# The first chunk's w_down product as seven products for eight, its sums on VectorE between the gate steps

## The chip, the cores and the metric

One NeuronCore of a Trainium2 chip runs the whole kernel. The metric is the time of one execution on the device in microseconds. Engines in the profile: PE is the tensor engine (PEld its weight loads), DVE is VectorE, ACT is ScalarE, POOL is GpSimd, SP the queue that issues most transfers. PE writes its results into banks of PSUM, from which the other engines take them.

## The reference, cut to what matters

```
xn = layernorm(x)                          # x: 2048 x 448
q  = xn @ wq                               # 16 heads of 256
s  = softmax(q k^T / 16) v  @ wo           # 512 keys, 8 kv heads
g  = silu((gelu(xn @ w_gate) * (xn @ w_up)) @ w_down)     # 1792 features
return x + s * g                           # bf16
```

The change touches only `(gelu(..) * (..)) @ w_down`: 2048 x 1792 by 1792 x 448, done in four chunks of 512 rows.

## The kernel before

The gate part is a loop of steps; a step makes two blocks of 128 features for 512 rows on PE (28 matmuls), then ScalarE takes the gelu and VectorE the multiply out of PSUM. Chunk 0 has steps 0 to 12, chunk 1 steps 14 to 26, and so on. Between steps stands a chunk's product with w_down. Three of the four chunks do it already as a 2 x 2 block product with seven block products for eight (Winograd's form): some block sums first, seven products, then combinations.

```python
def down(c, pairs):                      # chunk 0: the plain product, bf16
    for t4 in range(4):
        ...
        mms([(bank[b][:, 0:D], actT[:, c % 2, f, t4 * P:(t4 + 1) * P], wd[:, f, :], f == 0, f == NF - 1)
             for f in range(NF)], [b_wd] + b_actT[c % 2], (b_ps[b],))
        act(tmp[:, s, 0:D], bank[b][:, 0:D], ACT.Tanh, ..., scale=0.5)
        ...                              # gate on VectorE, store

def sum_wd(o, x, y):                     # one of four weight sums, 128 x 1568, fp16
    add("dve", wdt[o][0], wdt[x][0], wdt[y][0], ..., ALU.subtract)

def sum_act(c, k, i=None):               # one of four activation sums, in two halves i of feature blocks
    ...                                  # k = 0 is in place: right half of the rows becomes left - right

def down7(c, banks, g, b_g, order=(3, 6, 5, 4, 2, 1), then=None):
    ...
    A = lambda e, r: (lambda i: actTh[:, c % 2, e * NH + i, r * HC:(r + 1) * HC], b_actT[c % 2][e * NH:(e + 1) * NH])
    ...
    product(0, B1, A(0, 0))              # 14 matmuls of 128 x 224 each
    act(U2, bank[B1][:, 0:D], ACT.Copy, (b_ps[B1],), bU2, scale=F)
    for j in order:
        product(j, *what[j], j != 1)
    if then:
        then()
    plus(U2, bU2, B6, U2, bU2)           # six combinations on VectorE, then tanh and gate
    ...
```

Note the second element of `A(0, 0)`: the buffers that the first product is said to read are those of whole feature blocks, while it reads the left half of their rows.

The softmax here doesn't subtract the row's maximum and nothing guards it: scores larger than these inputs give would overflow.

## Time and profile before

| | us |
|---|---|
| median of 3 runs (lowest to highest) | 541.97 (541.92 to 542.07) |
| PE busy | 533.5 of a span of 540.6 |
| chunk 0: plain product, first matmul to next step | 10.70 |
| chunk 1: seven products, first matmul to next step | 9.49 |

PE is the bound from end to end; the prediction shows the lines. For stages I use three landmarks on PE: the first whole gate step (its first matmul on w_gate's last rows), the first attention product, and the last run of matmuls with w_o. Before, these stand at 12.02, 119.03 and 531.19 us. The profile's view of busy time in the two stretches between them (length; busy us and instructions of PE, PEld, DVE, ACT, POOL; clock; DMA share; GB/s):

```profile
12.02:119.03 107.01, 106.83 (x962) 55.79 (x960) 78.21 (x146) 60.66 (x95) 14.35 (x27) 1.00 0.61 137
119.03:531.19 412.16, 410.00 (x2883) 237.69 (x2907) 284.20 (x632) 246.01 (x672) 23.61 (x44) 1.00 0.50 104
```

I call them **head** (107.01 us) and **attention part** (412.16 us); the change edits only the head.

### The profile page before, as it was taken

The page shows a single profiled execution, that of the slowest core. Times are in us where ns is not written, and L with a number is a line of the kernel's source. Part 1 is how long each engine was busy: PE and PEld are TensorE (multiplying, and loading weights), DVE is VectorE, ACT ScalarE, POOL GpSimd, SP SyncE. Part 2 cuts the span into 40 slices and gives each one's busy share as a digit, 9 for nine tenths or more (in the row PEclk, how much of TensorE's full clock was granted, in tenths as well). Part 3 has the DMA queues.
Part 4 walks back from the last instruction along what each step waited for, and adds up shares of the span by engine and source line. Part 5 has one row for each costly group of instructions (what it writes and reads, how often), then busy time and mean ns, then how long its engine had stood idle before and what let it go on. Part 6 is the DMA issues. An engine that isn't in the chain of part 4 may idle for free.

```text
span 540.6 us, 10823 instructions
## 1 busy us (share of the span) xinstructions
PE 533.5 (99%) x4113; PEld 306.1 (57%) x4138; DVE 376.2 (70%) x825; ACT 313.3 (58%) x780; POOL 39.4 (7%) x78
## 2 busy tenths in 40 slices
PE   8999999999999999999999999999999999999997
PEld 5554457449644444984444469544444984444587
DVE  6673895799767757934875786367567934776775
ACT  5433854873658858116875860488488116876820
POOL 1130400000000010003001000120100003001010
PEclk9999999999999999999999999999999999999999
DMA  9569271921496788302781670076457402873731
GB/s 291 128 186 130 45 142 41 299 66 41 113 191 133 147 192 156 60 1 78 166 145 47 156 137 1 18 148 149 94 106 153 64 1 72 162 156 83 134 72 35
DMA packets 171604, 61.38 MB, mean 114 GB/s; under 512 B 155104, under 2 KB 168416, under 8 KB 171552
## 3 DMA queue, kind: packets, MB, share of 16 engines
q1 hardware_dynamic: 167488, 51.30, 44.5%
q0 software_dynamic: 3008, 8.72, 7.1%
q8 instruction: 33, 0.54, 0.4%
q10 hardware_dynamic: 1056, 0.66, 0.4%
q14 instruction: 19, 0.16, 0.1%
HBM read 19.76 MB, written 3.67 MB: 43 GB/s over the span
## 4 chain that ended last, share of the span: by engine, by line
PE 98%; issue 0%; DMA 0%; DVE 0%
PE bank L392 98%; DMA x<-in_A_x_dram 0%; DVE stats L439 0%; PE bank L490 0%; DVE xn L465 0%; DVE mv L442 0%; PE bank L509 0%; DVE xnT L898 0%; DVE xnT L386 0%; DVE rstd L459 0%
## 5 line engine op out<-in xcount | busy, mean ns | idle before, releaser
L844 ACT ACTIVATE p<-bank 128x512 f32<-128x512 f32 x256 | 150.6, 596 | 27.8 <-DVE pn L851 25.4
L392 PE MATMUL bank<-pT,va 128*128 128x512 bf16 x512 | 120.9, 379 | 0.0
L392 PE MATMUL bank<-kT,qT 128*128 128x512 bf16 x487 | 117.8, 379 | 2.3 <-ACT qT L383 1.0
L851 DVE TENSOR_SCALAR pn<-p,rden 128x512 bf16<-128x512 f32 x256 | 113.0, 483 | 8.2 <-DMA pT<-pn 3.9
L392 PE MATMUL bank<-xnT,wq 64*128 64x512 bf16 x768 | 94.9, 376 | 0.0
L392 PEld LDWEIGHTS bank<-kT,qT 128*128 128x128 bf16 x512 | 49.3, 98 | 61.7 <-issue 3.4
L392 PEld LDWEIGHTS bank<-pT,va 128*128 128x128 bf16 x512 | 49.6, 98 | 61.0 <-DMA pT<-pn 2.3
L392 PE MATMUL bank<-xnT,wgu 64*128 64x512 bf16 (+2 forms) x768 | 83.9, 350 | 0.1
L383 ACT ACTIVATE qT<-bank 128x512 bf16<-128x512 f32 x76 | 44.1, 596 | 51.8 <-PE bank L392 50.2
L829 DVE CAST qT<-bank 128x512 bf16<-128x512 f32 x52 | 34.8, 690 | 49.5 <-PE bank L392 49.5
L392 PEld LDWEIGHTS bank<-xnT,wq 64*128 64x128 bf16 x768 | 36.7, 94 | 46.3 <-ACT p L844 2.1
L392 PEld LDWEIGHTS bank<-xnT,wgu 64*128 64x128 bf16 x768 | 37.0, 94 | 36.8 <-issue 0.6
L848 DVE RECIPROCAL rden<-rsum 128x2 f32<-128x2 f32 x128 | 21.1, 165 | 47.0 <-ACT p L844 47.0
L844 ACT ACTIVATION_READ_ACCUMULATOR p<-bank 128x1 f32 x256 | 51.7, 202 | 0.0
L392 PE MATMUL bank<-wt,sr 128*128 128x224 f16 x512 | 50.0, 259 | 0.0
L383 ACT ACTIVATE gl<-bank 128x512 bf16<-128x512 f32 x56 | 33.1, 596 | 28.5 <-PE bank L392 26.1
L392 PEld LDWEIGHTS bank<-wt,sr 128*128 128x128 f16 x512 | 49.0, 98 | 0.4 <-ACT oTh L383 0.2
L869 DVE TENSOR_SCALAR oTh<-bank 128x512 f16<-128x512 f32 x62 | 42.3, 683 | 0.0
L383 ACT ACTIVATE oTh<-bank 128x512 f16<-128x512 f32 x66 | 38.9, 590 | 4.2 <-PE bank L392 4.2
L392 PE MATMUL bank<-wt,oTh 128*128 128x224 f16 (+1 forms) x416 | 38.4, 252 | 0.0
L392 PEld LDWEIGHTS bank<-wt,oTh 128*128 128x128 f16 x416 | 37.2, 98 | 0.9
L377 POOL DMA_DIRECT2D g<-g_all x14 | 7.6, 540 | 379.2 <-DVE xnT L386 255.3
(82 smaller groups left out, 403.6 us busy)
## 6 DMA issues: line engine op xcount, KB each, us to landing
wtb<-in_A_wo_dram POOLq DMA_DIRECT2D x4, 896.0 KB, 11.1
wq<-in_A_wq_dram SPq DMA_DIRECT2D x2, 1536.0 KB, 7.1
va<-in_A_v_cache_dram SPq DMA_DIRECT2D x8, 256.0 KB, 5.7
pT<-pn SPq DMA_TRANSPOSE x128, 2.8
xr<-in_A_x_dram POOLq DMA_DIRECT2D x15, 112.0 KB, 2.3
wd<-in_B_w_down_dram SPq DMA_DIRECT2D x1, 1568.0 KB, 7.4
g<-g_all POOLq DMA_DIRECT2D x14, 112.0 KB, 2.3
out_dram<-xr POOLq DMA_DIRECT2D x12, 112.0 KB, 2.1
```

Of the source, the lines that this page charges most:

```text
L377: K.op(q, lambda e, o=o, i=i: e.dma_start(o, i), reads, writes, dma=True, after=after)
L383: K.op("act", lambda e, o=o, i=i: e.activation(o, i, func, scale=scale), reads, writes)
L392: ins = e.matmul(o, lhsT=l, rhs=r, start=st, stop=sp, skip_group_check=True)
L829: K.op("dve", lambda v, s=s, b=b: v.tensor_copy(qT[:, s, 1, :], bank[b + 1]), (b_ps[b + 1],), (b_qT[s][1],))
L844: K.op("act", lambda e, b=b, r=r, z=z: e.activation(p32[:, z, :], bank[b], ACT.Exp, scale=att_scale, accum_out=rsum[:, r:r + 1]), (b_ps[b] ...
L848: K.op("dve", lambda e, r=r: e.reciprocal(rden[:, r - 1:r + 1], rsum[:, r - 1:r + 1]), b_rsum[r - 1:r + 1], b_rden[r - 1:r + 1])
L851: K.op("dve", lambda e, r=r - 1 + t, z=(n - 1 + t) % NP32, y=y, t=t: e.tensor_scalar(pn[:, y, t, :], p32[:, z, :], rden[:, r:r + 1], None, ...
L869: K.op("dve", lambda v, i=i, b=b: v.tensor_scalar(oTh[:, i, :], bank[b], WS, None, op0=ALU.mult), (b_ps[b],), (b_oT[i],))
```

## The change

Its intent: an eighth of the PE work of the last plain product goes, with the sums that this needs fitted into VectorE's free time between gate steps. The product moves from after step 18 to after step 26, so that the sums have time. The core of the diff:

```diff
-            o = actTh if c else actT
-            K.op("dve", lambda e: e.tensor_tensor(o[:, c % 2, f, :], bank[b + 1], gl[:, s, :], ALU.mult),
+            K.op("dve", lambda e: e.tensor_tensor(actTh[:, c % 2, f, :], bank[b + 1], gl[:, s, :], ALU.mult),
...
-        WD_CASTS = [(20, (j, e, n, i)) for ...]
-        DN_SUMS = [(24, sum_act, (1, k, 0)) for k in range(4)] + [
-            (30, sum_wd, x) for x in ((4, 4, 0), (5, 2, 4), (6, 5, 0), (3, 1, 5))] + [(34, sum_act, (1, k, 1)) for k in range(4)]
-        DOWN_AT = {NF + 5: 0, 39: 1}
+        WD_CASTS = [(16, (j, e, n, i)) for ...]
+        WD_SUMS = [(18, (4, 4, 0)), (20, (5, 2, 4)), (22, (6, 5, 0)), (24, (3, 1, 5))]
+        ACT_SUMS = [(n, (c, k, i)) for c, i, ns in ((0, 0, (10, 11, 19, 21)), (0, 1, (23, 23, 25, 25)),
+                                                    (1, 0, (30, 32, 34, 34)), (1, 1, (36, 36, 38, 38)))
+                    for k, n in enumerate(ns)]
+        DOWN_AT = {27: 0, 39: 1}
...
-            if ln_t[0] < 8 or n >= 12:
+            if ln_t[0] < 8 or 12 <= n and ln_t[0] < 12 or n >= 28:
                 ln_a()
...
-                    down(DOWN_AT[n + 1], cur)
+                def norms():
+                    for f in (ln_a, ln_a, ln_b, ln_b):
+                        f()
+                end = down7(DOWN_AT[n + 1], (...), (...), b_g2x, then=norms if n < 28 else None)
```

In a step the loop emits the weight sums of that step first and its activation sums after them.

## The prediction

> **What bounds the kernel now.** I read first the busy times and the chain that ended last, then the tensor engine's timeline around the product that is changed, then the vector engine's, because that is where the new work goes.
>
> The page of the kernel before (busy us, share of the span, instructions; then the chain by engine):
>
> ```profile
> PE 533.5 (99%) x4113; PEld 306.1 (57%) x4138; DVE 376.2 (70%) x825; ACT 313.3 (58%) x780; POOL 39.4 (7%) x78
> ...
> PE 98%; issue 0%; DMA 0%; DVE 0%
> ```
>
> The kernel is tensor-engine bound nearly from end to end. So a microsecond taken from PE's queue is a microsecond of time, unless PE then has to wait for somebody, and what another engine does costs nothing until PE waits for it. The tensor engine's timeline around the first chunk's w_down product (start, length, what), and around the second chunk's, which is already done as seven products:
>
> ```profile
> 36.53 1.48 PE L392 MATMUL bank<-xnT,wgu 64*128 64x512 bf16 x12
> 37.93 10.77 PE L392 MATMUL bank<-wd,actT 128*128 128x448 bf16 x56
> 48.63 0.82 PE L392 MATMUL bank<-xnT,wgu 64*128 64x512 bf16 x6
> ...
> 77.56 1.46 PE L392 MATMUL bank<-xnT,wgu 64*128 64x512 bf16 x12
> 78.96 1.52 PE L392 MATMUL bank<-wdh,actTh 128*128 128x224 f16 x14
> ...
> 88.45 0.82 PE L392 MATMUL bank<-xnT,wgu 64*128 64x512 bf16 x6
> ```
>
> From its first matmul to the first of the next gate step, the plain form takes 48.63 - 37.93 = 10.70 us and the seven-product form 88.45 - 78.96 = 9.49 us, neither with a wait in or ahead of it. Gate steps follow each other every 3.02 us (two feature blocks a step; step 18 ends at 37.93).
>
> **What the Trainium skill says.** "TensorE: Matmul & The Clock Gate", section "Wait — 56ns, not 53.3ns?", gives N/2.4 GHz + 2.5 ns between warm matmuls of N columns. That is an estimate of 56 x 189.2 = 10.59 us and 98 x 95.8 = 9.39 us, a difference of 1.20 us; the trace has 10.70 and 9.49, so it agrees, and I use the trace's difference of 1.21 us.
> "VectorE: DVE Perf Modes", section "The perf-mode tier table", has tensor_tensor at two elements a cycle for 16-bit operands in SBUF and at one with an operand in PSUM. The trace agrees: a weight sum of 1568 half-precision elements takes 0.96 us, a gate multiply of 512 elements from PSUM 0.69.
> "SBUF — State Buffer", section "Who interferes with whom", says that a VectorE instruction with two SBUF inputs holds off a GpSimd one that reads SBUF until it is over. This matters for layer norms, whose reciprocal deviation is two tiny GpSimd operations. GpSimd in the kernel before, without and with such a sum beside it:
>
> ```profile
> 57.59 0.22 POOL L449 TENSOR_SCALAR ve<-mv 128x1 f32<-128x1 f32 x1 [2.15 <-DVE mv L442]
> 57.90 0.57 POOL L451 TENSOR_TENSOR rstd<-ve,nhalf 128x1 f32<-128x1 f32 x1
> 60.61 0.57 POOL L449 TENSOR_SCALAR ve<-mv 128x1 f32<-128x1 f32 x1 [2.15 <-DVE mv L442]
> 61.26 0.57 POOL L451 TENSOR_TENSOR rstd<-ve,nhalf 128x1 f32<-128x1 f32 x1
> ```
>
> The first operation goes from 0.22 to 0.57 us where an activation sum of 0.66 us runs beside it, and VectorE pays for it in turn:
>
> ```profile
> 60.34 0.18 DVE L442 BATCH_NORM_AGGREGATE mv<-stats 128x2 f32<-128x6 f32 x1
> 60.44 0.66 DVE L386 TENSOR_TENSOR actTh<-actTh 128x1024 f16<-128x1024 f16 x1
> 61.05 0.69 DVE L559 TENSOR_TENSOR actTh<-bank,gl 128x512 f16<-128x512 f32 x1
> 61.94 0.61 DVE L465 TENSOR_SCALAR xn<-x,mv,rstd 128x448 bf16<-128x448 bf16 x2 [0.20 <-POOL rstd L451]
> ```
>
> The normalization starts 0.84 us after the end of that sum. The trace agrees with the page.
>
> **The change, part by part.**
> *Removed:* 56 matmuls of 448 columns, four tanh and four gate products behind them. *Added:* 98 matmuls of 224 columns. On PE this is **-1.21 us**. The product also moves from after gate step 18 to after step 26, which costs nothing on PE: the same steps run before or after.
> *ScalarE:* the eight casts of w_down move from steps 20 to 28 to steps 16 to 22, two a step. The trace shows such a step as two gelus and two casts, next gelu 3.02 us later with hardly a gap; so the casts fit. Net new are about three operations of 0.55 us. No PE wait from here.
> *VectorE:* the eight sums of the first chunk's activations are new, about 4 x 0.66 + 4 x 0.55 = 4.8 us; six combinations of 0.62 us and as many gates as before are added, so DVE's total rises by some 8.5 us of 540. What matters is where: the four weight sums (0.96 us) now lie in steps 18 to 24 together with six of the new sums and still with the layer norm of tile 11. VectorE has 3.02 us a step, of which the two gate multiplies take 1.2.
>
> So I walked VectorE's queue from step 18 on, in the order in which the changed kernel emits it, with start-to-start times from the trace where VectorE is behind (these lines give them):
>
> ```profile
> 68.35 0.68 DVE L386 TENSOR_TENSOR sd<-actTh,sd 128x1024 f16<-128x1024 f16 x1
> 68.95 0.96 DVE L386 TENSOR_TENSOR wdh<-wdh 128x1568 f16<-128x1568 f16 x1
> ...
> 73.26 1.28 DVE L559 TENSOR_TENSOR actTh<-bank,gl 128x512 f16<-128x512 f32 x2
> 74.46 0.96 DVE L386 TENSOR_TENSOR wdt<-wdh,wdt 128x1568 f16<-128x1568 f16 x1
> 75.34 0.55 DVE L386 TENSOR_TENSOR actTh<-actTh 128x768 f16<-128x768 f16 x1
> ```
>
> Multiply pair 1.20, weight sum 0.88, activation sum of 1024 elements 0.59, normalization of one tile 0.51. Up to step 18 nothing differs from before, and there the trace has VectorE starting its last statistics of tile 11 at 40.21 and their aggregate at 40.86. Then:
> - 40.96: first weight sum, done at 41.92, in front of GpSimd's square root for tile 11. First multiply of step 20 from 41.85 to 42.45.
> - Normalization of tile 11: 41.92 + 0.84 = 42.76, so 0.3 us are lost. It ends at 43.27, the second multiply at 43.87.
> - Second weight sum to 44.75, activation sum to 45.34, multiplies of step 22 to 46.54, third weight sum to 47.42, activation sum to 48.01, multiplies of step 24 to 49.21, fourth weight sum to 50.09.
> - Only now the first half-sum of the second half of blocks (in place, 0.55 us): it is done at **50.64**.
>
> Gate step 26 ends on PE at 37.93 + 4 x 3.02 = 50.01. The first of the seven products reads rows of the activation tile whose buffer that last sum writes (the dependency is kept per feature block, not per half), so it can't start before 50.64 plus a semaphore and a weight load (98 ns in the trace), about 50.8. PE waits **about 0.75 us** there. The later products have slack: the sums for the fourth to the sixth are done by about 53.5, the fourth starts at 50.8 + 3 x 1.34 = 54.8. The banks are free in time too: the multiplies of step 20 end at 43.9, and their second pair of banks is wanted at 44.8.
> *Layer norms of two tiles between:* four statistics operations and four normalizations, some 2.8 us with waits on GpSimd, between 53.5 and 56.8 on VectorE, while PE works on the products; the combinations can't start before the fourth product ends (about 56.2). They end at about 59.8, the products at 60.3. Hidden.
> *Second chunk:* its sums now come two steps later, in the two steps before its product, but those steps hold no weight sums: 1.2 + 1.1 us of 3.02. The one that the first product waits for ends a microsecond early. Hidden.
>
> Sum: -1.21 + 0.75 = -0.46 us, so 541.97 - 0.46 = **541.5 us**.
>
> **Rivals.**
> 1. *No wait at all:* the whole 1.21 us arrive, 540.75. For it: the second chunk's product has no wait ahead of it. Against: that one had its weight sums over five steps early, and the walk above would have to be off by 0.65 us over 17 instructions.
> 2. *The wait eats everything or more:* 1.2 us or above, 542.0 to 542.4. For it: VectorE is behind from step 18 to the product, so each further hitch (GpSimd again, a gelu late for its multiply) adds in full. Against: ScalarE has its gelus done before VectorE asks, and only one tile is normalized in that stretch.
> 3. *The delay spreads to gate steps:* VectorE frees a bank too late and PE stands in steps 24 or 26. The margin is 0.9 us at the tightest, so I give it little; it would not add to the wait before the product but move part of it.
> 4. *Something downstream:* later tiles, weight loads and the attention part keep their order, and shift by half a microsecond. I expect no change above 0.1 us.
>
> **Range and chances.** The three runs of before differ by 0.15 us, so noise is small. The term in doubt is the wait, 0.75 us with perhaps 0.2 to 1.2; from that 541.0 to 542.0. A change of 2% would be 10.8 us, nine times the whole gain on PE, so anything but "within 2%" would take a wait that nothing here hints at.
>
> **What would show it.** In the changed profile: the seven products about 9.5 us from first to last; ahead of them a gap of 0.5 to 1 us on PE, released by an activation sum on VectorE; VectorE without idle time from about 41 to 53.6 but for some 0.3 us before tile 11's normalization, released by GpSimd; its total up by 8 to 9 us; PE's busy time down by 1.2. Wrong would be: no gap there (then 540.8), gaps inside gate steps 20 to 26, or a gap after the products, where the combinations would hold the banks.

## The result, and the profile after

| | before | after |
|---|---|---|
| median us, first measurement (6 runs each) | 542.06 (541.92 to 544.26) | 542.05 (541.71 to 542.30) |
| ratio of fast runs, 95% interval | | 0.9987 (0.9967 to 1.0006) |
| span of the profiled run | 540.6 | 539.9 |

A ratio is the mean time of one kernel's fast runs over that of the other's in the same rounds, so it is not quite the ratio of the medians. The difference is far inside the 2% that would count as faster or slower, and the interval holds 1. Two of the six runs of before took 544.2 us; the mean of its other four is 542.00, so the 0.9987 rests on these two. The median lies a hair above the predicted range of 541.0 to 542.0, the ratio times 541.97 (541.3) inside it. The size of a gain under one microsecond can't be read from the total; it can from the traces. The page of the changed kernel:

```profile
PE 532.9 (99%) x4155; PEld 310.9 (58%) x4180; DVE 383.8 (71%) x839; ACT 314.0 (58%) x782; POOL 40.1 (7%) x78
...
PE 92%; DVE 2%; ACT 2%; DMA 2%; issue 1%; ACTq 0%
```

42 more matmuls and as many weight loads, 7.6 us more on VectorE, PE's busy time down by 0.6 us only, and a chain that is no longer PE's alone. PE's timeline at the new place of the product:

```profile
48.52 1.48 PE L394 MATMUL bank<-xnT,wgu 64*128 64x512 bf16 x12
50.62 1.52 PE L394 MATMUL bank<-wdh,actTh 128*128 128x224 f16 x14 [0.63 <-DVE actTh L388]
...
60.12 0.82 PE L394 MATMUL bank<-xnT,wgu 64*128 64x512 bf16 x6
```

The products take 60.12 - 50.62 = 9.50 us. A step's last twelve matmuls take 1.40 us to the next group's start where nothing waits, so PE was ready at 49.92 and stood 0.70 us, released by an activation sum. VectorE's timeline shows that sum at the end of a queue:

```profile
42.64 0.61 DVE L467 TENSOR_SCALAR xn<-x,mv,rstd 128x448 bf16<-128x448 bf16 x2 [0.24 <-POOL rstd L453]
...
49.13 0.96 DVE L388 TENSOR_TENSOR wdt<-wdh,wdt 128x1568 f16<-128x1568 f16 x1
50.01 0.55 DVE L388 TENSOR_TENSOR actTh<-actTh 128x768 f16<-128x768 f16 x1
```

In this trace everything stands 0.10 us earlier than in the other from the start on. The sum ends at 50.56; the walk had 50.64, which is 50.54 with that shift; the steps between agree within 0.03 us too, so the sum is not right by errors that cancel. GpSimd's first operation for tile 11 is stretched beside the first weight sum, as foretold:

```profile
41.03 0.85 POOL L451 TENSOR_SCALAR ve<-mv 128x1 f32<-128x1 f32 x1 [2.15 <-DVE mv L444]
```

Now both stretches after:

```profile
11.92:118.43 106.51, 105.69 (x1004) 60.54 (x1002) 85.63 (x160) 61.49 (x97) 14.93 (x27) 1.00 0.63 137
118.43:530.98 412.55, 410.18 (x2883) 237.69 (x2907) 284.37 (x632) 245.89 (x672) 23.67 (x44) 1.00 0.49 104
```

The head is 0.50 us shorter, as worked out (-1.20 + 0.70). But the attention part, which no line of the change touches and which has the same number of instructions, is 0.39 us longer. And from the last landmark to the end it is 8.92 us against 9.41. Start, head, attention part and end make -0.10 - 0.50 + 0.39 - 0.49 = -0.70, the difference of the spans (which are listed to a tenth, so the ends are good to 0.05 us). So two things needed experiments: whether the wait in the head is what I said, and why untouched stages moved.

The attention part differs at single places. Between them PE's groups follow each other to 0.01 us in both traces. Before and after, near 419 us:

```profile
417.39 1.89 PE L392 MATMUL bank<-kT,qT 128*128 128x512 bf16 x8
419.11 1.89 PE L392 MATMUL bank<-pT,va 128*128 128x512 bf16 x8
```

```profile
416.78 1.89 PE L394 MATMUL bank<-kT,qT 128*128 128x512 bf16 x8
418.80 1.90 PE L394 MATMUL bank<-pT,va 128*128 128x512 bf16 x8
```

The product of probabilities and values follows the scores after 1.72 us before and 2.02 after. It waits for the transposed probabilities, a transfer.

### The profile page after: what moved, and what is told of

Read it like the earlier page. It is cut to its first block, busy times and chain, and to the rows that moved or that the text cites. A ratio compares the mean times of both kernels' runs of the same rounds, so it can differ in the third digit from the quotient of the medians.

```text
span 539.9 us, 10920 instructions
## 1 busy us (share of the span) xinstructions
PE 532.9 (99%) x4155; PEld 310.9 (58%) x4180; DVE 383.8 (71%) x839; ACT 314.0 (58%) x782; POOL 40.1 (7%) x78
## 4 chain that ended last, share of the span: by engine, by line
PE 92%; DVE 2%; ACT 2%; DMA 2%; issue 1%; ACTq 0%
PE bank L394 91%; ACT p L830 2%; DMA pT<-pn 2%; DVE pn L837 1%; PE bank L511 1%; DVE actTh L560 0%; DVE rden L834 0%; DVE wdt L388 0%; PE bank L492 0%; ACT gl L385 0%; DVE actTh L388 0%; DVE sd L388 0%; ACT oTh L385 0%; DVE xnT L884 0%; DVE gl L424 0%
## 5 line engine op out<-in xcount | busy, mean ns | idle before, releaser
L560 DVE TENSOR_TENSOR actTh<-bank,gl 128x512 f16<-128x512 f32 x56 | 37.4, 688 | 11.9 <-PE bank L394 6.4
```

The lines of the kernel that those rows point to most:

```text
L560: K.op("dve", lambda e: e.tensor_tensor(actTh[:, c % 2, f, :], bank[b + 1], gl[:, s, :], ALU.mult), (b_ps[b + 1], b_gl[s]), (b_actT[c % 2] ...
```

## The experiments

Twelve runs were made, four of them repeats of a kernel, and all were correct. No difference comes near 2%; what is read below are the intervals and the traces. For each I give its edit against the changed kernel, unless said, and the table at the end has the stages of every trace.

### r_after: the changed kernel again

No edit.

> The changed kernel again, unedited, for the sign of the change. Theory: PE's queue up to the attention part is 0.50 us shorter (1.20 us fewer in the products, 0.70 us wait ahead of them), and the attention part's small waits for transposed probabilities and the transfers at start and end jitter by some tenths; so the mean is 0.3 to 0.7 us below before, 541.4 to 541.7 us. Rival: later waits give the gain back systematically, so equal means within 0.1 us. In the trace: wait of 0.70 us ahead of the seven products, products 9.5 us.

Measured: 542.79 us median of 5 (541.87 to 543.57) against 542.40, ratio 1.0004 (0.9990 to 1.0017). The trace has the wait and the 9.5 us again, head 106.50 us. Its attention part is 414.32 us: near 264 us one product of probabilities and values is 1.4 us late, the one near 419 us 0.9. So the head was as expected, the mean was not: it fits the rival better. The kernel before ran from 541.95 to 543.04 us beside it, so it spreads too.

### e1_sum_first: the awaited half-sum ahead of the fourth weight sum

```diff
+            if n == 24:
+                sum_act(*ACT_SUMS.pop(0)[1])
             while WD_SUMS and n >= WD_SUMS[0][0]:
```

> The first half-sum that the first product waits for is put ahead of the fourth weight sum, all else equal. Theory (VectorE's queue is the wait): the sum ends 0.88 us earlier, at about 49.7 us, before gate step 26 ends at 49.9; the gap ahead of the products goes from 0.70 to under 0.1 us, and the kernel is 0.6 to 0.7 us faster than the changed one, 1.1 to 1.2 below before. Rival (the gap is set by something else, a bank or a transfer): gap stays at 0.7. Second rival (gain absorbed later): gap gone, time the same as the changed kernel's.

VectorE and PE in its trace:

```profile
49.05 0.55 DVE L388 TENSOR_TENSOR actTh<-actTh 128x768 f16<-128x768 f16 x1
49.51 0.96 DVE L388 TENSOR_TENSOR wdt<-wdh,wdt 128x1568 f16<-128x1568 f16 x1
```

```profile
48.44 1.47 PE L394 MATMUL bank<-xnT,wgu 64*128 64x512 bf16 x12
49.84 1.51 PE L394 MATMUL bank<-wdh,actTh 128*128 128x224 f16 x14
```

The gap is gone; the head is 105.80 us, 1.21 below before and 0.70 below the changed kernel. Median 541.26 us, ratio to before 0.9985 (0.9972 to 0.9997). Swapping two instructions of VectorE gives the whole gain on PE: the wait was VectorE's queue.

### e2_half_dep: the first product depends on what it reads

```diff
+        b_left = [[K.buf() for f in range(NF)] for i in range(2)]
...
-                (b_ps[b + 1], b_gl[s]), (b_actT[c % 2][f],))
+                (b_ps[b + 1], b_gl[s]), (b_actT[c % 2][f], b_left[c % 2][f]))
...
-            product(0, B1, A(0, 0))
+            product(0, B1, (A(0, 0)[0], b_left[0][:NH]) if c == 0 else A(0, 0))
```

> The first product of the first chunk depends on the left halves of its activation rows alone, which it reads, not on the in-place sum in the right halves; VectorE's order is that of the changed kernel. Theory: the gap ahead of the products goes from 0.70 us to under 0.1, since the next product needs only the fourth weight sum, which ends at about 50.1 us, 1.1 us before it is wanted; time 0.6 to 0.7 us below the changed kernel, as with the sum put first. Rival (VectorE is late for the later products too): the gap reappears ahead of the second or third product.

Gap gone again (the products start 1.41 us after the step's last twelve matmuls), head 105.80 us, no gap ahead of the second or third product. VectorE's order was the changed kernel's; so PE had waited for a sum whose result the first product does not read. The time, 541.54 us, ratio 0.9993 (0.9981 to 1.0006), came out less clear than expected: its trace has a product 1.55 us late near 264 us, attention part 414.04 us.

### e3_extra_sum: one weight sum twice

```diff
                 sum_wd(*WD_SUMS.pop(0)[1])
+                if not WD_SUMS:
+                    K.op("dve", ...same operation again..., after=[K.ops[-1]])
```

> The fourth weight sum is done twice, the second after the first, so VectorE has one more operation of 0.96 us in front of the half-sum. Theory: the wait ahead of the products grows by 0.9 to 1.0 us to about 1.65 us, and the time rises by as much against the changed kernel. Rival (VectorE has slack and the wait is for something else): gap and time unchanged.

```profile
51.88 1.51 PE L394 MATMUL bank<-wdh,actTh 128*128 128x224 f16 x14 [1.63 <-DVE actTh L388]
```

The wait grew from 0.63 to 1.63 us in the profile's count, the head to 107.50 us, 1.00 over the changed kernel. 543.30 us, ratio 1.0018. VectorE's time ahead of that sum goes through one to one, as expected.

### r_before: the kernel before, as if it were a change

> The kernel before, unedited, submitted as if it were a change, for a second trace of it and for the spread of its own times. Theory: first gate step to first attention product takes 112.86 us again (within 0.1 us), and the attention part differs from its first trace by single late transposes of up to 1.5 us, as the traces of the changed kernels did among each other; ratio 1.000 with an interval as wide as the others'. Rival: its attention part is free of such waits (within 0.3 us of the first trace), so the waits belong to the change.

Ratio 1.0002 (0.9990 to 1.0015), 542.39 us. Head 107.01 us, the same to a hundredth. The attention part is 412.47 us, 0.31 from its first trace, with several products 0.1 to 0.2 us late and none by more; the one near 419 us is on time. The 0.31 us fall on the line of 0.3 that the rival had drawn, so the run does not decide: small late products are not the change's alone, while large ones and that one near 419 us had by now shown only in traces of changed kernels. No trace was kept of the slowest runs of before (544.2 us, in the first measurement and in a later set of rounds), so large ones may occur there too.

### e4_norms_later: layer norms not between the products and their combinations

```diff
-                            ..., b_g2x, then=norms if n < 28 else None)
+                            ..., b_g2x, then=None)
```

> The layer norms of two tiles are not put between the products and their combinations; tiles 12 to 15 are normed in the gate steps from 28 on. Theory (they lie beside the products and are hidden): PE's way from the first gate step to the first attention product is the changed kernel's 112.3 us within 0.1 us, and the wait ahead of the products stays 0.70 us. Rival (they delay the combinations, which hold the banks, or their place was needed for a later step): that stretch differs by 0.2 us or more, and a wait shows after the products or in a gate step.

The wait ahead of the first chunk's products stayed at 0.70 us, so the norms there are hidden. But the head became 107.30 us, 0.80 longer, because of a wait ahead of the *second* chunk's products:

```profile
79.07 1.51 PE L394 MATMUL bank<-wdh,actTh 128*128 128x224 f16 x14 [0.73 <-DVE actTh L388]
```

The rival is right about the stretch. Four norms instead of two now lie in steps 28 to 36, among the second chunk's sums, and VectorE falls behind there as it did in the first chunk. 543.75 us, ratio 1.0026 (1.0007 to 1.0045). The odd place of the two norms is needed.

### e5_late11: tile 11 normalized behind the sums

```diff
-            ln_b()
+            if not 20 <= n < 28:
+                ln_b()
...
-                    for f in (ln_a, ln_a, ln_b, ln_b):
+                    for f in (ln_b, ln_a, ln_a, ln_b, ln_b):
```

> The normalization of tile 11 moves from gate step 20 to behind the sums of step 26, where the products already run. VectorE loses 0.51 us of work and the 0.24 us wait for GpSimd from the queue ahead of the half-sum. Theory: that sum ends 0.75 us earlier, the wait ahead of the products goes from 0.70 us to under 0.1, and the stretch from the first gate step to the first attention product is 111.6 us, as with the sum put first. Rival (a later gelu or cast holds VectorE instead, so that time taken out upstream is not passed on): the wait shrinks by less than 0.5 us.

```profile
50.91 1.52 PE L394 MATMUL bank<-wdh,actTh 128*128 128x224 f16 x14 [0.19 <-DVE actTh L388]
```

```profile
42.45 1.28 DVE L560 TENSOR_TENSOR actTh<-bank,gl 128x512 f16<-128x512 f32 x2
44.02 0.98 DVE L388 TENSOR_TENSOR wdt<-wdh 128x1568 f16<-128x1568 f16 x1 [0.29 <-ACT wdh L385]
```

The theory failed here. The wait is 0.27 us (start 50.91, last twelve matmuls from 49.24) and the head 106.07, so 0.43 of the 0.75 us came through. VectorE, now early, waits 0.29 us for ScalarE's cast of the weights for the second weight sum. (PE's first whole gate step came 0.5 to 0.8 us later in this run than in those told so far; the head is counted from behind that.) 541.78 us, ratio 0.9990 (0.9975 to 1.0005).

### What moved the attention part: e6, e7 and e8

By now all seven traces of changed kernels had the product near 419 us late by 0.3 us or more, neither of before. The page's list of transfer queues has two of the kind "instruction": q8 with 33 transfers of 16,384 bytes, together 0.54 MB, and q14 with 19 of 8,192 bytes. The Trainium skill, "Runtime: NRT & Kernel Launch", section "Instruction fetch mechanics", says that an engine's sequencer fetches its coming instructions over a DMA queue of its own, in blocks of 16 KiB, which are 256 instructions. The trace agrees in the size for q8, not for q14. PE's 4113 matmuls and 4138 loads fill 32 blocks of 256, against 33 transfers in q8: this estimate is the reason to take q8 for PE's. Whose q14 is stays open. The change adds 84 instructions ahead of the attention part, so there each such transfer comes earlier against the work. The list of transfers in a window from 5 to 3 us ahead of that product, before and after:

```profile
q1 hardware_dynamic: 1056, 0.26, 58.1%
pT<-pn SPq DMA_TRANSPOSE x2, 3.0
```

```profile
q1 hardware_dynamic: 1140, 0.28, 128.2%
q8 instruction: 1, 0.02, 3.2%
pT<-pn SPq DMA_TRANSPOSE x2, 4.3
```

The columns are packets, MB and the packets' time as a share of all 16 engines' (packets in flight count, so it can pass 100%). After, an instruction transfer (queue q8) stands in the window, and the transposes issued there land after 4.3 us in place of 3.0. It takes 1.0 us in the trace. That is no single case: of the 1792 transposes in the 14 kept traces, the 265 with a q8 transfer starting between their issue and their landing land after a median of 4.2 us, the other 1527 after 2.7, and every trace shows this alike (4.0 to 4.3 against 2.7). Three experiments move the transfers without touching the work.

**e6_before_pad42**, an edit of the kernel *before*:

```diff
-        warm(9, 2, QC)
+        ...                    # pad(n): n matmuls of 32 columns
+        warm(5, 2, QC)
+        pad(46)
```

> The kernel before, with 42 more matmuls in the idle start of PE (five 512-column warm-up matmuls and 46 of 32 columns in place of nine): as many as the change adds, with no other edit. In all seven traces of changed kernels one product of probabilities and values, near 419 us, starts 0.3 us late or more, in both of the kernel before never; and in them a 16 KB instruction transfer starts 3 to 5 us ahead of it, where before has it 2 us behind. Theory (84 more instructions on PE move its instruction transfers onto that transposed block): this kernel has that product 0.3 us late too, with the way from the first gate steps to attention 107.0 us as before, and is 0.2 to 0.6 us slower than before. Rival (the delay comes from the seven products' shift of the stages against each other, or from the stores): the product is on time, time as before.

The product near 419 us is late by 0.33 us, with an instruction transfer 4.0 us ahead of it. Those near 264 (1.5 us), 381 (0.3) and 467 us (0.4) are late too, so the attention part is 2.0 to 2.3 us longer than in the two traces of before (its 414.68 us less the 0.22 explained under the table of stages). Its list of groups for the worst of them:

```profile
266.28 1.90 PE L392 MATMUL bank<-pT,va 128*128 128x512 bf16 x8 [1.36 <-DMA pT<-pn]
```

So the kernel before, with nothing but 42 more matmuls at its start, shows the changed kernel's late products; the stages' order and VectorE's new work are not needed. 544.32 us, ratio 1.0037 (1.0018 to 1.0056), more than I expected: 1.0 us of it is a later first gate step (13.04 us), the pad's own cost. That later start is not what makes the products late: e8 below starts 0.7 us late and has them on time.

**e7_sum_pad8**, the kernel with the half-sum first:

```diff
-        warm(9, 2, QC)
+        warm(8, 2, QC)
+        pad(9)
```

> The kernel with the half-sum first, with 8 more matmuls of 32 columns at the start, which moves PE's later instruction transfers earlier by about 16 instructions, 1.7 us in the attention part. Theory: the transfer that stood 3.9 us ahead of the product near 418 us stands more than 5 us ahead, and that product is on time; the kernel is 0.3 us faster than without the pad, some 1.4 us below before, unless another transfer now lands on another block. Rival: the product stays 0.3 us late.

A miss: the transfer near 415 us did not move (414.5 us against 414.1), though those near 262 and 374 came 3 us earlier. The product near 418 us stayed late (0.48 us), with the transfer 4.2 us ahead. It says only that so small a pad does not shift all transfers alike. 541.75 us, ratio 0.9994.

**e8_sum_pad86**, the same with 86 more matmuls, so 256 instructions more than before, one whole transfer:

```diff
-        warm(9, 2, QC)
+        warm(3, 2, QC)
+        pad(92)
```

> The kernel with the half-sum first, with 86 more matmuls at the start (three of 512 columns and 92 of 32 in place of nine). With the change's 42 that makes 128 matmuls, and with a weight load each 256 instructions or one 16 KB instruction transfer more, so the transfers should lie in the attention part as they do in the kernel before. Theory: the product near 418 us is on time (1.72 us after the one before it), none of those near 264 and 378 us is late by over 0.2 us, and from the first attention product to the last output matmul it takes 412.2 to 412.5 us as in the two traces of before, against 412.5 to 414.3 in those of the changed kernels. The start may lose up to 1 us, as with the other long pad, so the total tells little. Rival (the stages' shift against each other or the stores make that product late): it stays 0.3 us late.

The list of transfers 5 to 3 us ahead of that product, which is now on time (1.73 us after the scores), as are those near 264 and 378 us:

```profile
q1 hardware_dynamic: 1056, 0.26, 61.5%
q14 instruction: 1, 0.01, 1.3%
...
pT<-pn SPq DMA_TRANSPOSE x2, 3.1
```

No q8 there, only one of the small transfers of q14; from 112 us on its transfers lie within about 1 us of those of one of the two traces of before. Attention part 412.51 us, a hair over the expected 412.5, with smaller late products elsewhere (0.3 us near 213 us). The start cost 0.7 us, so the total is 542.79 us, ratio 1.0004.

In the eleven traces with a transfer 3.8 to 4.3 us ahead of the product near 419 us it is late by 0.29 to 0.90 us; in the three without, it is on time. Near 264 us it is the same: five traces have a transfer 3.1 to 4.3 us ahead and are late by 0.33 to 1.55 us, the others have none there and are on time. The small transfers of q14 are no rival: at both places one stands 1.7 to 3.1 us ahead in all 14 traces, late or not.

Two limits belong to this. A transfer ahead does not suffice: of the 868 products of probabilities and values counted (62 in each trace), 119 have a q8 transfer that starts 3.0 to 4.5 us ahead, and 19 of these are late by 0.25 us or more; of the 749 others, 2 are. What else it takes at those two places was not tested. And the count of instructions alone does not fix the place: in the three traces of the same changed kernel the transfer near 262 us starts at 262.8, 260.3 and 262.9 us, and only the second has the late product there.

The end moves with it. The kernel before has an instruction transfer at 537.0 us, in the middle of its last output stores; the changed one has its last at 532.8. The stores in the last 6 us, before and after (KB each, us to landing):

```profile
out_dram<-xnT ACTq DMA_DIRECT2D x1, 56.0 KB, 2.9
out_dram<-xnT SPq DMA_DIRECT2D x1, 28.0 KB, 2.6
```

```profile
out_dram<-xnT ACTq DMA_DIRECT2D x1, 56.0 KB, 1.6
out_dram<-xnT SPq DMA_DIRECT2D x1, 28.0 KB, 1.5
```

The end takes 9.4 to 9.6 us in the three traces with the old count of instructions, or 256 more, and 8.9 to 9.0 in the eleven others, e6 among them. So this half microsecond is not the products' doing either.

### e1_again and r_after_again, on the same chip

Copies of e1_sum_first and of the changed kernel.

> The kernel with the half-sum first once more, for its time on other rounds: 1.2 us less up to the attention part in every trace, 0.3 us late near 418 us, sometimes a block late by more; so 0.5 to 1.0 us below before in the mean (541.2 to 541.7).

541.56 us median, ratio to before 0.9985 (0.9973 to 0.9997), head 105.80 us: as expected.

> The changed kernel once more on the same chip as the two others: 0.50 us less up to the attention part, late blocks as in its other traces, so a mean within 0.4 us of before, and 0.4 to 1.0 us above the kernel with the half-sum first. Rival: both alike.

542.76 us median (541.32 to 544.10), ratio 1.0004 (0.9989 to 1.0020). As expected within its width, and above the kernel with the half-sum first by 1.2 us in the median. Its trace was of its fastest run, with an attention part of 412.14 us.

### The stages of all traces

| trace | first gate step at | head | attention part | end |
|---|---|---|---|---|
| before / r_before | 12.02 / 11.93 | 107.01 / 107.01 | 412.16 / 412.47 | 9.41 / 9.59 |
| after / r_after / r_after_again | 11.92 / 12.02 / 11.95 | 106.51 / 106.50 / 106.50 | 412.55 / 414.32 / 412.14 | 8.92 / 8.96 / 8.91 |
| e1_sum_first / e1_again | 11.85 / 12.15 | 105.80 / 105.80 | 412.45 / 413.77 | 8.90 / 8.98 |
| e2_half_dep | 11.89 | 105.80 | 414.04 | 8.97 |
| e3_extra_sum | 12.19 | 107.50 | 412.39 | 8.92 |
| e4_norms_later | 11.85 | 107.30 | 412.19 | 8.96 |
| e5_late11 | 12.65 | 106.07 | 412.25 | 8.93 |
| e6_before_pad42 | 13.04 | 106.78* | 414.68* | 8.90 |
| e7_sum_pad8 | 12.10 | 105.58* | 413.10* | 8.92 |
| e8_sum_pad86 | 12.71 | 105.81 | 412.51 | 9.37 |

The end is the span as the run lists it, to a tenth, less the last landmark: good to 0.05 us.

*In these two the first record of the attention part is there, in the others it is missing; 0.22 us of the attention part belong to the head.

## Why the prediction was right or wrong

- *1.21 us on PE:* right, 1.20 to 1.21; the head without a wait (e1, e2) is 1.21 us shorter. PE's busy time falls by 1.14 us in the head, but by 0.6 in all, not by the 1.2 foretold; the rest comes back outside the head and was not looked into.
- *The wait ahead of the products, 0.75 us, from VectorE's queue:* right, 0.70 us in three traces. e1 and e2 remove it in two independent ways, e3 lengthens it by 1.00 us. The 0.3 us lost to GpSimd at tile 11 measured 0.24 and stands in the trace; e5 took it out only with the normalization, so its share alone was not tested. The trace agrees with what the Trainium skill's "SBUF — State Buffer", section "Who interferes with whom", says of such pairs: GpSimd's operation ends at 41.88 us, 0.08 after the weight sum beside it.
- *Casts on ScalarE cause no wait on PE:* right for the changed kernel (its net new work was two operations and 0.7 us, less than the three of 0.55 us expected), but e5 shows that they stand close behind: they end 0.29 us after VectorE would want them, once tile 11 is out of the way.
- *Layer norms between, second chunk's sums:* hidden, as worked out; e4 shows that the place for the norms is what keeps the second chunk's sums hidden.
- *VectorE's total, "8 to 9 us" up:* it rose by 7.6, a small miss. (The prediction counts six new activation sums in steps 18 to 24; by the kernel and the trace four lie there and two in step 26. The walk has the right order, so nothing hangs on it.)
- *Rival 4, "I expect no change above 0.1 us" downstream:* **wrong, and the step that failed.** Untouched stages moved: the attention part by 0.0 to +2.2 us in the three traces of the changed kernel (the two of before differ by 0.3), the end by -0.5. e6 and e8 show, with one trace each, that the count of PE's instructions is enough for the late product near 419 us and for the end: the change adds 84, and that moves the instruction transfers onto other transposes and off the last stores. The large delays near 264 us come and go from trace to trace of one kernel.
- *541.5 us:* the head's -0.5 was right; the total's median came out 0.55 above, beside a before that was itself 0.09 higher than in the three runs that the forecast started from. That the first ratio, 0.9987, fits the forecast is in part luck, given the two runs of before at 544.2 us; the 0.5 us that the end gained was not foreseen either. Over three sets of rounds the ratios to before are 0.9987, 1.0004 and 1.0004, so the mean gain of the whole kernel is not resolved from zero.

What stays open: how often in many runs a product is late by 1 us or more (the changed kernel's times run from 541.3 to 544.1 us, one trace per set shows where), and by what path an instruction transfer lengthens the landing of the transposes, which no run isolates. If a version is wanted, e1_sum_first is the best: 0.9985 to before twice, both intervals below 1. Against the changed kernel in the same rounds its mean is 1.25 and 1.04 us lower; no interval was taken for that pair, and with eight more matmuls at the start (e7) the ratio to before was 0.9994, not clear of 1.

## What to carry to other kernels

When PE is the bound and another engine's queue feeds it, walk that queue in emission order with start-to-start times: it foretold a wait of 0.7 us to within 0.05, and the cure was to emit the awaited sum ahead of a longer one that is wanted later. Freed time is passed on only as far as the next engine behind allows (0.43 of 0.75 us in e5). And below one microsecond compare stages, not totals, over more than one trace: a change of instruction count alone moved this kernel's untouched end by as much as the change gained in the head.

## What the Trainium skill lacked or had wrong

- "Runtime: NRT & Kernel Launch", section "Instruction fetch mechanics": its 16 KiB blocks fit queue q8 (33 of 16,384 bytes), but a second queue of the same kind, q14, moved 8,192 bytes at a time (19 of them), which it doesn't have. It calls the cost of the blocks mostly hidden and doesn't say what they do to other transfers. Here the small transposing transfers land after a median of 4.2 us with such a block beside them and 2.7 without, and at two places of the attention part this goes with 0.3 to 1.55 us of delay of the product that waits for them; 42 more matmuls at the start moved blocks there (e6).
- "TensorE: Matmul & The Clock Gate", section "Wait — 56ns, not 53.3ns?": nothing wrong; the estimates worked out from its spacing, 10.59 and 9.39 us for the two forms, are 0.1 us short of the trace's 10.70 and 9.49 to the next step, and the difference between the forms was right.
- "SBUF — State Buffer", section "Who interferes with whom": right here, but it has no length for this pair: beside a weight sum of 0.94 us GpSimd's first operation took 0.85 us in place of 0.22.
